# Attention with an off-by-one softmax, then a soft mixture of experts: the extra term of the denominator added by TensorE in PSUM, the half chunk of x stored without zero blocks, x transposed 448 wide, and q and k copied by ScalarE for every sixth pair

## The chip, the cores and the metric

The kernel runs on one core of one Trainium2 chip. That core has TensorE (PE in the profile, with its weight loads as PEld), VectorE (DVE), ScalarE (ACT), GpSimd (POOL) and SyncE (SP, which here only issues transfers). The metric is device microseconds for one execution. Lower is better.

## The reference, cut to what matters

```python
# q, k, v: batch 8, 12 heads, 448 tokens, 64 wide
scores = scale * q @ k.T
m = max(scores, -1);  e = exp(scores - m)
attn = e / (sum(e, -1) + exp(-m) + 1e-9)      # the off-by-one term is exp(-m)
x = (attn @ v), heads side by side            # 3584 tokens x 768
logits = x @ phi                              # 32 slots: 8 experts x 4
d = softmax(logits over all tokens);  slot_input = d.T @ x
slot_out[e] = relu(slot_input[e] @ w1[e]) @ w2[e]     # 768 -> 1024 -> 768
c = softmax(logits over the slots);  out = c @ slot_out
```

Each head has 448 tokens, which is three chunks of 128 and a half chunk of 64. Much of the kernel's shape, and of this change, comes from that half chunk.

## The kernel before

**Pairs.** The 96 heads are worked through as 48 pairs of heads, `s` or `n` from 0 to 47; a batch has six pairs, and three pairs are a group. The even head of a pair lies in partitions 0 to 63 and the odd one in 64 to 127. The order of all instructions on every engine is the order in which the Python lists them: there is no scheduler, and each engine works through its own list.

**One pair.** `T` (L214) transposes q and k into one PSUM tile with 28 transposes of 64x64, and ScalarE (L227) or VectorE (L229) copies the result to SBUF; which of them is set by `n < 6 or pl == 0`, where `pl` is the pair's place in its group. `A1` and `A` compute scores with the query in the partitions (L268, L256), and VectorE takes the maximum of each row (L270, L259). `W1` to `W3`, once a group, negate the maxima on GpSimd, transpose them on TensorE (L297, L298), copy them with ScalarE (L303), and compute exp(-m) into `ec` (L306, L309). `AB` and `Bk` compute the scores again with the key in the partitions (L354, L332), subtract the maximum by a second matmul into the same PSUM bank (L358, L335), and ScalarE exponentiates (L360, L338). `AB` also carries the `A1` matmuls of a later pair between its own. `AV` (L393) multiplies the exponentials with v, which has a column of ones behind its 64 columns, so each of the seven 65-wide results holds its own row sum in column 64. For the three full chunks of queries the stationary tile is 128x128; for the half chunk (`qs = [3]`) it is 128x64, the two heads going to the two halves of the PSUM partitions.

**Normalising.** `N1` (L405) copies the 455 columns to `ubuf`, on ScalarE for the first 44 pairs. `N2` adds 1e-9 and exp(-m) to the seven row sums with one VectorE instruction (L414), takes the reciprocal (L415), and GpSimd multiplies it into x: the three full chunks (L419), then for the half chunk a pair of masked reciprocals (L423) and a 128x128 product (L424). The mask makes a block in which each head's 64 columns are zero in the 64 partitions that belong to the other head. `PX` (L445) transposes x with four matmuls of 128x128, the last of them against `ident2`, two identities of 64 stacked, and ScalarE copies 512 columns to `xT` (L451).

**Per batch.** `P(b)` lists steps for the slot softmax that are put between the pairs of the next batch: `l_mm` (L471, logits: 6 parts of the model width by 4 chunks), `s_mm` (L539, slot inputs: 6 by 4 matmuls and 4 for the sums), a fade of the running sum when the maximum moves, and `c_turn` (L544 to L549), which stores the row softmax and the reciprocal of its sum. The last batch's steps, `last`, stand behind the pairs.

**One turn of the main loop** is, in TensorE's order: `AB(s,0)`, `AB(s,1)`, `AV(s-1)` for key chunks 2 and 3, a batch step, `AV(s-1)` for the half chunk of queries, `N1(s-1)`; then `AB(s,2)`, `Bk(s,3)`, `T(s+6)`, once a group `W2` and `W3`, `AV(s)` for key chunks 0 and 1, a batch step, `PX(s-2)`, `N2(s-1)`. All transfers from HBM are issued by GpSimd between its computations. Behind the pairs come the two expert layers, a selection, and 56 output matmuls (L793) whose results are scaled and stored. The tiles of the attention share one long SBUF tile `R`; expert weights are loaded over its parts once those are done with.

Of the kernel before, what the change touches and what calls it, by code (L numbers as in the profile page):

```python
# [25 lines left out]
NP = 3  # L26
# [5 lines left out]
def kernel(  # L32
# [35 lines left out]

    ident = const.tile([128, 128], BF16, name="ident")
    identf = const.tile([128, 128], F32, name="identf")  # L70
    ident2 = const.tile([128, 128], BF16, name="ident2")
# [3 lines left out]
    halfm = const.tile([128, 2], F32, name="halfm")  # L75

    NQK, NE, VPN, NATV = 7, 5, HG * 4 * VS, HG * 4 * D
    sizes = [("nq0", 2 * NP * S), ("nq1", 2 * NP * S), ("nv", NATV), ("qk6", 2 * S), ("wm1", 512),  # L80
             ("qk0", 2 * S), ("qk1", 2 * S), ("qk2", 2 * S), ("wm0", 512), ("qk3", 2 * S), ("vp0", VPN),
             ("qk4", 2 * S), ("x0", 4 * DD), ("qk5", 2 * S), ("e2", NE * 2 * S), ("e1", S), ("vp1", VPN),
             ("xT", KC * 512), ("x1", 4 * DD)]
    at_, n_ = {}, 0
    for nm, z in sizes:
        at_[nm] = n_
# [8 lines left out]
    xb = [part(f"x{i}", 0, 4 * DD).rearrange("p (i d) -> p i d", i=4) for i in range(2)]  # L95
    xT = part("xT", 0, KC * 512).rearrange("p (j s) -> p j s", j=KC)

    halves = [("w1", e) for e in range(E)] + [("w2", e) for e in range(E)]
    w_sb, w_col = {}, {}
# [43 lines left out]
    with ExitStack() as at:  # L143
# [33 lines left out]
        load(1, "k")  # L177


        for h in range(2):  # L180
            nc.vector.tensor_add(ident2[:, 64 * h:64 * h + 64], ident[:, 0:64], ident[:, 64:128])
        nc.vector.tensor_copy(identf, ident)
        nc.gpsimd.memset(sel, 0.0)
        for base in (0, 64):
# [5 lines left out]
        nc.vector.memset(halfm, 0.0)  # L190
        for hl in range(2):
            nc.vector.memset(halfm[64 - 64 * hl:128 - 64 * hl, hl:hl + 1], 1.0)
        for t in wm:
            nc.vector.memset(t, 0.0)
        for t in vp:
# [18 lines left out]
        def T(n):  # L214
            g, pl = divmod(n, NP)
            ps = psA.tile([128, 2, S], BF16, tag="a", name="ps_t")
            for a in range(2):
                src = nat["qk"[a], g]
                for tok in range(7):
                    for hl in range(2):  # L220

                        c = kcol(hl, tok) if a else (2 * tok if tok < 4 else 2 * tok - 7) * 64
                        r = slice(64 * hl, 64 * hl + 64)
                        nc.tensor.transpose(ps[r, a, c:c + 64], src[r, pl, tok * D:(tok + 1) * D], ident[r, r])  # L224
            t = qk_t[n % NQK]
            if n < 6 or pl == 0:
                nc.scalar.copy(t, ps)  # L227
            else:
                nc.vector.tensor_copy(t, ps)  # L229
            qkT[n] = t  # L230
# [62 lines left out]
        def W2(g):  # L293
            w = wm[g % 2]
            ps = pb_("ps_m")
            for i in range(3):
                nc.tensor.matmul(ps[:, i * 128:(i + 1) * 128], w[:, i, :], ident, start=True, stop=True)  # L297
            nc.tensor.matmul(ps[:, 384:448], w[:, 3, :], ident2[:, 0:64], start=True, stop=True)  # L298
            st["ps_m"] = ps

        def W3(g):
            t = psm.tile([128, S], BF16, tag="mT", name="mT")
            nc.scalar.copy(t, st["ps_m"][:, 0:S])  # L303
            mT[g] = t
            e = psm.tile([128, NP, 7], F32, tag="ec", name="ec", bufs=3)
            nc.scalar.activation(e[:, :, 0:6].rearrange("p l (i h) -> p i l h", i=3),  # L306
                                 ngm[g][:, 0:18].rearrange("p (i l h) -> p i l h", i=3, h=2),
                                 AF.Exp, scale=scale)
            nc.scalar.activation(e[:, :, 6], ngm[g][:, 18:21], AF.Exp, scale=scale)  # L309
            ec[g] = e  # L310


        def Bk(n, i, c=0):
# [94 lines left out]
        def N2(n):  # L408
            g, pl = divmod(n, NP)
            b, pb = divmod(n, PB)  # L410
            u = us[n]
            eng = nc.gpsimd if on_pool(n) else nc.vector
            rec = psm.tile([128, 7], F32, tag="rec", name="rec", bufs=3)
            nc.vector.scalar_tensor_tensor(rec, u[:, :, D], 1e-9, ec[mg(n)][:, pl, :], op0=ALU.add, op1=ALU.add)  # L414
            nc.vector.reciprocal(rec, rec)  # L415
            x = xb[b % 2]
            c = pb * 128
            rec2 = psm.tile([128, 2], F32, tag="rec2", name="rec2", bufs=3)
            eng.tensor_mul(  # L419
                x[:, 0:3, c:c + 128].rearrange("p i (h d) -> p i h d", h=2),  # L420
                u[:, 0:6, 0:D].rearrange("p (i h) d -> p i h d", h=2),
                rec[:, 0:6].rearrange("p (i h) -> p i h", h=2).unsqueeze(3).to_broadcast([128, 3, 2, D]))
            eng.tensor_scalar(rec2, halfm, rec[:, 6:7], None, op0=ALU.mult)  # L423
            eng.tensor_mul(  # L424
                x[:, 3, c:c + 128].rearrange("p (h d) -> p h d", h=2),
                u[:, 6, 0:D].unsqueeze(1).to_broadcast([128, 2, D]),
                rec2.unsqueeze(2).to_broadcast([128, 2, D]))

# [9 lines left out]
        def PX(n):  # L438
            b, pb = divmod(n, PB)
            x, c = xb[b % 2], slice(pb * 128, pb * 128 + 128)  # L440
            two = n == NPAIR - 1
            pss = [pb_("ps_x") for _ in range(1 + two)]
            for i in range(4):
                o = (i % 2 if two else i) * 128
                nc.tensor.matmul(pss[i // 2 if two else 0][:, o:o + 128], x[:, i, c], ident if i < 3 else ident2,  # L445
                                 start=True, stop=True)
            if two:
                nc.scalar.copy(xT[:, pb, 0:256], pss[0][:, 0:256])
                nc.vector.tensor_copy(xT[:, pb, 256:512], pss[1][:, 0:256])
            else:  # L450
                nc.scalar.copy(xT[:, pb, :], pss[0])  # L451

# [5 lines left out]
        def P(b):  # L458
# [7 lines left out]
            def l_mm(js):  # L466
                if js[0] == 0:
                    v["ps_l"] = pa([128, 4, NS], F32, "ps_l")
                for j in js:
                    for i in range(4):  # L470
                        nc.tensor.matmul(v["ps_l"][:, i, :], xT[:, j, i * 128:(i + 1) * 128], phi_sb[:, j, :],  # L471
                                         start=(j == 0 and i == 0), stop=(j == KC - 1), skip_group_check=True)

            def t_mm(js):
                if js[0] == 0:
                    v["ps_t"] = pa([128, 128], F32, "ps_lT")
                for j in js:
                    for i in range(4):
                        nc.tensor.matmul(v["ps_t"][32 * i:32 * i + 32, :], phi_sb[:, j, :],
                                         xT[:, j, i * 128:(i + 1) * 128], start=(j == 0), stop=(j == KC - 1),  # L480
                                         skip_group_check=True)

            def l_ev():
# [48 lines left out]
            def s_mm(j0=0, j1=KC + 1):  # L532
                ps = pa([128, j1 - j0, NS], F32, "ps_s")
                for j in range(j0, j1):
                    for i in range(4):

                        w = x[:, i, j * 128:(j + 1) * 128] if j < KC else \
                            ones[:, int(i == 3):int(i == 3) + 1].to_broadcast([128, 128])
                        nc.tensor.matmul(ps[:, j - j0, :], w, v["cd"][:, 4 + i, :], start=(i == 0), stop=(i == 3))  # L539
                v["ps_s"] = ps  # L540

            def c_turn():
                ps = pa([128, 128], BF16, "ps_ct")
                nc.tensor.transpose(ps, flat(v["cd"][:, 0:4, :]), ident)  # L544
                nc.vector.tensor_copy(cT[:, b // 2, :, b % 2, :], ps.rearrange("p (h j) -> p h j", h=2))
                r = crec[:, b, :]
                nc.vector.reduce_sum(r, v["cd"][:, 0:4, :], axis=AX.X)
                nc.vector.tensor_scalar(r, r, 1e-9, None, op0=ALU.add)
                nc.vector.reciprocal(r, r)  # L549

            def s_add():
                if b:
# [82 lines left out]
        for s in range(NPAIR):  # L635
            for y in range(2):
# [40 lines left out]
                if y == 0:  # L677
                    if 0 <= s - 1:
                        for i in range(4):
                            AV(s - 1, i, [3])  # L680
                        N1(s - 1)
                        if not on_pool(s - 1):
                            N2(s - 1)
                else:
                    if 0 <= s - 1 and on_pool(s - 1):
                        N2(s - 1)
# [34 lines left out]
        for i in range(3):  # L721
            AV(n, i, [3])
        AV(n, 3, range(4))
        load_second(0, 4)
        N1(n)
        N2(n)
# [160 lines left out]
```

## Time and profile before

| What | Value |
|---|---|
| Median of 3 runs | 311.84 us (309.37 to 312.33) |
| The profiled execution's own time | 310.7 us |
| Its span, first to last instruction | 308.9 us |
| Mean granted TensorE clock | 0.964 |
| TensorE busy / weight loads busy | 275.6 us (89%) / 159.0 us (51%) |
| VectorE busy | 257.2 us (83%) |
| ScalarE busy | 249.3 us (81%) |
| GpSimd busy | 202.7 us (66%) |

A busy time is the union of an engine's instruction intervals. The end of a matmul in the trace is modelled and includes its way through the array, so that two matmuls overlap in the rows; what a matmul costs in a row of them is read from the distance between their starts. That distance is called a slot in the prediction. "128\*64" in a row is the stationary tile, rows by columns; "128x65" is the result.

### The profile page before, as it was taken

To read this page: it belongs to the slowest core of one execution; us is meant where nothing else is said; L and a number is where in the kernel's file an instruction comes from. 1 tells how busy PE (TensorE), PEld (TensorE's weight loads), DVE (VectorE), ACT (ScalarE), POOL (GpSimd) and SP (SyncE) were. 2 spreads that over 40 slices of the span, in tenths; PEclk is the share of its full clock that TensorE was granted. 3 is DMA by queue.
4 is the path that set the end of the run, shared out by engine and by line. 5 is a ranking of instruction groups with operands and counts; after the bars stand their busy time and mean duration, and the time that the engine had idled before them with its cause. 6 is when DMAs were issued, how large, how long until landed. Compare 5 with 4: busy or idle time off the path is not lost.

```text
span 308.9 us, 12205 instructions
## 1 busy us (share of the span) xinstructions
PE 275.6 (89%) x5067; PEld 159.0 (51%) x5068; DVE 257.2 (83%) x607; ACT 249.3 (81%) x549; POOL 202.7 (66%) x403
## 2 busy tenths in 40 slices
PE   2899999999999999999999999999999899994810
PEld 1434456565666656665566566656665556451200
DVE  4778999999999999999999999999999566536930
ACT  2357599999999999999999999999999997236810
POOL 8682769788788878896889788879584863000000
PEclk9999999999999999999999999999999999999555
DMA  6999499999999999999999999999971999937997
GB/s 88 149 128 202 64 205 150 198 182 205 163 196 157 210 169 198 155 203 149 149 164 186 177 186 169 196 177 203 166 110 17 144 126 204 337 128 260 415 439 312
DMA packets 49350, 57.44 MB, mean 186 GB/s; under 512 B 2832, under 2 KB 41488, under 8 KB 48912
## 3 DMA queue, kind: packets, MB, share of 16 engines
q0 software_dynamic: 45536, 42.52, 90.1%
q1 hardware_dynamic: 3760, 14.16, 11.5%
q8 instruction: 39, 0.64, 0.8%
q14 instruction: 15, 0.12, 0.1%
HBM read 88.18 MB, written 14.16 MB: 331 GB/s over the span
## 4 chain that ended last, share of the span: by engine, by line
PE 50%; DVE 30%; ACT 7%; issue 4%; POOL 4%; DMA 1%; DVEq 0%; POOLq 0%
DVE mx L270 15%; PE ps_av L393 11%; PE ps_a L268 6%; PE ps_t L224 6%; PE ps_b L354 5%; PE ps_b L358 4%; DVE mx L250 3%; DVE mx L259 3%; PE ps_b L332 3%; PE ps_a L246 2%; DVE W L801 2%; DVE R L229 2%; PE ps_x L445 2%; ACT R L227 2%; PE ps_so L764 2%
## 5 line engine op out<-in xcount | busy, mean ns | idle before, releaser
L270 DVE TENSOR_REDUCE mx<-ps_a 128x1 f32<-128x448 f32 x248 | 136.6, 613 | 5.3 <-PE ps_a L268 5.1
L360 ACT ACTIVATE R<-ps_b 128x448 bf16<-128x448 f32 x272 | 131.0, 573 | 1.1 <-PE ps_b L358 0.8
L268 PE MATMUL ps_a<-R 64*128 64x448 bf16 x248 | 80.5, 352 | 1.8 <-DVE mx L270 1.8
L354 PE MATMUL ps_b<-R 64*128 64x448 bf16 x272 | 73.9, 353 | 0.9
L358 PE MATMUL ps_b<-mT,sel 64*128 64x448 bf16 x272 | 70.6, 350 | 0.0
L393 PEld LDWEIGHTS <-R 128*128 128x128 bf16 (+1 forms) x1536 | 50.5, 101 | 30.5 <-issue 26.4
L393 PE MATMUL ps_av<-R 128*128 128x65 bf16 (+1 forms) x1536 | 64.9, 196 | 0.1
L419 POOL TENSOR_TENSOR R<-ubuf,rec 128x384 bf16<-128x384 f32 x44 | 36.3, 825 | 37.9 <-DVE rec L415 23.4
L224 PEld LDWEIGHTS <-R 64*64 64x64 bf16 x1344 | 31.1, 113 | 19.2 <-issue 7.8
L338 ACT ACTIVATE R<-ps_b 128x448 bf16<-128x448 f32 x64 | 36.0, 579 | 5.9 <-PE ps_b L335 5.9
L224 PE MATMUL ps_t<-ident,R 64*64 64x64 bf16 x1344 | 32.0, 198 | 5.9 <-DMA R<-in_q_dram 4.3
L451 ACT CAST R<-ps_x 128x512 bf16<-128x512 f32 x47 | 28.1, 598 | 5.7 <-PE ps_x L445 5.7
L259 DVE TENSOR_REDUCE mx<-ps_a 128x1 f32<-128x448 f32 x48 | 29.6, 616 | 0.6 <-PE ps_a L256 0.3
L358 PEld LDWEIGHTS <-sel 64*128 64x128 bf16 x272 | 21.5, 94 | 14.9 <-issue 5.3
L268 PEld LDWEIGHTS <-R 64*128 64x128 bf16 x248 | 23.1, 94 | 9.8
L405 ACT COPY ubuf<-ps_av 128x455 f32<-128x455 f32 x44 | 25.2, 573 | 3.0 <-PE ps_av L393 2.8
L227 ACT COPY R<-ps_t 128x896 bf16<-128x896 bf16 x20 | 18.4, 922 | 11.3 <-PE ps_t L224 11.0
L250 DVE TENSOR_REDUCE mx<-ps_a 128x1 f32<-128x448 f32 x40 | 22.6, 618 | 4.3 <-PE ps_a L246 3.9
L332 PE MATMUL ps_b<-R 64*64 64x448 bf16 (+1 forms) x112 | 22.7, 386 | 0.0
L335 PE MATMUL ps_b<-mT,sel 64*64 64x448 bf16 (+1 forms) x112 | 21.5, 366 | 0.0
L424 POOL TENSOR_TENSOR R<-ubuf,rec 128x128 bf16<-128x128 f32 x44 | 17.5, 398 | 3.7
L354 PEld LDWEIGHTS <-R 64*128 64x128 bf16 x272 | 17.2, 94 | 4.7 <-issue 0.2
(132 smaller groups left out, 454.0 us busy)
## 6 DMA issues: line engine op xcount, KB each, us to landing
W<-in_moe_w_dram POOLq DMA_DIRECT2D x22, 768.0 KB, 9.5
R<-in_v_dram POOLq DMA_DIRECT2D x32, 192.0 KB, 4.6
out_dram<-W SPq DMA_DIRECT2D x2, 2688.0 KB, 10.3
R<-in_q_dram POOLq DMA_DIRECT2D x15, 336.0 KB, 7.4
R<-in_k_dram POOLq DMA_DIRECT2D x15, 336.0 KB, 8.5
wd<-in_moe_w_dram POOLq DMA_DIRECT2D x8, 384.0 KB, 10.0
R<-wd SPq DMA_DIRECT2D x8, 384.0 KB, 8.6
R<-in_moe_w_dram POOLq DMA_DIRECT2D x2, 768.0 KB, 8.3
```

The lines of the kernel that those rows point to most:

```text
L224: nc.tensor.transpose(ps[r, a, c:c + 64], src[r, pl, tok * D:(tok + 1) * D], ident[r, r])
L250: nc.vector.reduce_max(mx[g][:, c:c + 1], pss[hl][:, 0:S], axis=AX.X)
L259: nc.vector.reduce_max(mx[g][:, c:c + 1], ps[:, 0:S], axis=AX.X)
L268: nc.tensor.matmul(ps[:, 0:S], t[r, 0, i * 128:(i + 1) * 128], t[r, 1, :], start=True, stop=True)
L270: nc.vector.reduce_max(mx[g][:, c:c + 1], ps[:, 0:S], axis=AX.X)
L332: nc.tensor.matmul(outs[hl], t[rs[hl], 1, cols], t[rs[hl], 0, :], start=True, stop=False)
L338: nc.scalar.activation(e, p[:, 0:S], AF.Exp, scale=scale)
L354: nc.tensor.matmul(ps[hl][:, 0:S], t[rs[hl], 1, cols], t[rs[hl], 0, :], start=True, stop=False)
L358: nc.tensor.matmul(ps[hl][:, 0:S], sel[rs[hl], h:h + 1].to_broadcast([64, 128]), mT[mg(n)][rs[hl], :], start=False, stop=True)
L360: nc.scalar.activation(e[:, hl, :], ps[hl][:, 0:S], AF.Exp, scale=scale)
L393: nc.tensor.matmul(o, eT[n, i, hl][:, qc], vp[g % 2][:, 2 * pl + hl, i, 0:W65], start=(i == 0 and u == 0 and hl == 0), stop=(i == 3), skip ...
L419: eng.tensor_mul(x[:, 0:3, c:c + 128].rearrange("p i (h d) -> p i h d", h=2), u[:, 0:6, 0:D].rearrange("p (i h) d -> p i h d", h=2), rec[: ...
```

## The change

Seven edits, made together:

1. `N2` no longer adds exp(-m). A new function `D1` adds it in PSUM: two f32 matmuls per pair with the f32 identity as the stationary tile, one moving the six columns of the full chunks, one the column of the half chunk, accumulated onto the row sums that `AV` left there. It stands between the last `AV` of a pair and its `N1`.
2. `W3` computes exp(-m) with one ScalarE instruction in place of two, and GpSimd adds 1e-9 to it.
3. The half chunk of x is stored 64 wide with no zeros (`xh`), by one GpSimd instruction in place of two.
4. Where that half chunk is the stationary operand it is now taken as two tiles: in `PX` and `s_mm` two 64x64 ones in place of one 128x128; in `l_mm` the 64 columns of `xT` twice as 128x64, once for each half of the PSUM partitions. `t_mm` moves the 64 columns twice.
5. `xT` is 448 wide in place of 512, and ScalarE copies 448 columns.
6. q and k of a pair are copied by ScalarE when `n % 6 == 0` (was: `n % 3 == 0`), else by VectorE, from pair 6 on.
7. The 1e-9 and the reciprocal of `c_turn` are done once for all batches, behind the pairs. Constants that only the mask needed are gone, and the parts of `R` move a little (a pad of 352 keeps what follows in its place within 32 elements).

```diff
-             ("qk4", 2 * S), ("x0", 4 * DD), ("qk5", 2 * S), ("e2", NE * 2 * S), ("e1", S), ("vp1", VPN),
-             ("xT", KC * 512), ("x1", 4 * DD)]
+             ("qk4", 2 * S), ("x0", 7 * DD // 2), ("pad", 352), ("qk5", 2 * S), ("e2", NE * 2 * S), ("e1", S), ("vp1", VPN),
+             ("xT", KC * S), ("x1", 7 * DD // 2)]
...
-            if n < 6 or pl == 0:
+            if n < 6 or n % 6 == 0:
                 nc.scalar.copy(t, ps)
...
-            e = psm.tile([128, NP, 7], F32, tag="ec", name="ec", bufs=3)
-            nc.scalar.activation(e[:, :, 0:6].rearrange("p l (i h) -> p i l h", i=3),
-                                 ngm[g][:, 0:18].rearrange("p (i l h) -> p i l h", i=3, h=2),
-                                 AF.Exp, scale=scale)
-            nc.scalar.activation(e[:, :, 6], ngm[g][:, 18:21], AF.Exp, scale=scale)
+            e = psm.tile([128, 21], F32, tag="ec", name="ec", bufs=3)
+            nc.scalar.activation(e, ngm[g], AF.Exp, scale=scale)
+            nc.gpsimd.tensor_scalar(e, e, 1e-9, None, op0=ALU.add)
             ec[g] = e
+
+        def D1(n):
+            pl, e = n % NP, ec[mg(n)]
+            d = av[n][:, 0:7 * W65].rearrange("p (s c) -> p s c", c=W65)[:, :, D]
+            nc.tensor.matmul(d[:, 0:6].rearrange("p (i h) -> p i h", h=2), identf,
+                             e[:, 0:18].rearrange("p (i c) -> p i c", i=3)[:, :, 2 * pl:2 * pl + 2],
+                             start=False, stop=True, skip_group_check=True)
+            nc.tensor.matmul(d[:, 6:7], identf, e[:, 18 + pl:19 + pl], start=False, stop=True, skip_group_check=True)
...
-            nc.vector.scalar_tensor_tensor(rec, u[:, :, D], 1e-9, ec[mg(n)][:, pl, :], op0=ALU.add, op1=ALU.add)
-            nc.vector.reciprocal(rec, rec)
+            nc.vector.reciprocal(rec, u[:, :, D])
...
-            eng.tensor_scalar(rec2, halfm, rec[:, 6:7], None, op0=ALU.mult)
-            eng.tensor_mul(
-                x[:, 3, c:c + 128].rearrange("p (h d) -> p h d", h=2),
-                u[:, 6, 0:D].unsqueeze(1).to_broadcast([128, 2, D]),
-                rec2.unsqueeze(2).to_broadcast([128, 2, D]))
+            eng.tensor_scalar(xh[b % 2][:, pb, :], u[:, 6, 0:D], rec[:, 6:7], None, op0=ALU.mult)
...
-            for i in range(4):
+            for i in range(3):
                 o = (i % 2 if two else i) * 128
-                nc.tensor.matmul(pss[i // 2 if two else 0][:, o:o + 128], x[:, i, c], ident if i < 3 else ident2,
+                nc.tensor.matmul(pss[i // 2 if two else 0][:, o:o + 128], x[:, i, c], ident, start=True, stop=True)
+            for hl in range(2):
+                r, o = slice(64 - 64 * hl, 128 - 64 * hl), 128 if two else 384
+                nc.tensor.matmul(pss[-1][64 * hl:64 * hl + 64, o:o + 64], xh[b % 2][r, pb, :], ident[r, r],
                                  start=True, stop=True)
...
-                nc.scalar.copy(xT[:, pb, :], pss[0])
+                nc.scalar.copy(xT[:, pb, :], pss[0][:, 0:S])
...
-                    for i in range(4):
-                        nc.tensor.matmul(v["ps_l"][:, i, :], xT[:, j, i * 128:(i + 1) * 128], phi_sb[:, j, :],
-                                         start=(j == 0 and i == 0), stop=(j == KC - 1), skip_group_check=True)
+                    for i in range(5):
+                        r = slice(0, 128) if i < 3 else slice(64 * i - 192, 64 * i - 128)
+                        nc.tensor.matmul(v["ps_l"][r, min(i, 3), :], xT[:, j, 128 * min(i, 3):min(128 * i + 128, S)],
+                                         phi_sb[:, j, :], start=(j == 0 and i == 0), stop=(j == KC - 1),
+                                         skip_group_check=True)
...
+                        if j < KC and i == 3:
+                            for hl in range(2):
+                                r = slice(64 - 64 * hl, 128 - 64 * hl)
+                                nc.tensor.matmul(ps[64 * hl:64 * hl + 64, j - j0, :], xh[b % 2][r, j, :],
+                                                 v["cd"][r, 7, :], start=False, stop=True, skip_group_check=True)
+                            continue
...
-                nc.vector.tensor_scalar(r, r, 1e-9, None, op0=ALU.add)
-                nc.vector.reciprocal(r, r)
...
                         for i in range(4):
                             AV(s - 1, i, [3])
+                        D1(s - 1)
                         N1(s - 1)
...
         AV(n, 3, range(4))
+        D1(n)
         load_second(0, 4)
...
         last[3]()
+        nc.vector.tensor_scalar(crec, crec, 1e-9, None, op0=ALU.add)
+        nc.vector.reciprocal(crec, crec)
```

More of the change, by code (lines that the diff above doesn't have):

```diff
@@ L70 @@
     identf = const.tile([128, 128], F32, name="identf")
-    ident2 = const.tile([128, 128], BF16, name="ident2")
+    ident2 = const.tile([128, 64], BF16, name="ident2")
     ones = const.tile([128, 2], BF16, name="ones")
@@ L74 @@
     phi_sb = const.tile([128, KC, NS], BF16, name="phi_sb")
-    halfm = const.tile([128, 2], F32, name="halfm")
     NQK, NE, VPN, NATV = 7, 5, HG * 4 * VS, HG * 4 * D
@@ L94 @@
     wm = [part(f"wm{i}", 0, 512).rearrange("p (i c) -> p i c", i=4) for i in range(2)]
-    xb = [part(f"x{i}", 0, 4 * DD).rearrange("p (i d) -> p i d", i=4) for i in range(2)]
-    xT = part("xT", 0, KC * 512).rearrange("p (j s) -> p j s", j=KC)
+    xb = [part(f"x{i}", 0, 3 * DD).rearrange("p (i d) -> p i d", i=3) for i in range(2)]
+    xh = [part(f"x{i}", 3 * DD, DD // 2).rearrange("p (j d) -> p j d", d=D) for i in range(2)]
+    xT = part("xT", 0, KC * S).rearrange("p (j s) -> p j s", j=KC)
     halves = [("w1", e) for e in range(E)] + [("w2", e) for e in range(E)]
@@ L177 @@
         load(1, "k")
-        for h in range(2):
-            nc.vector.tensor_add(ident2[:, 64 * h:64 * h + 64], ident[:, 0:64], ident[:, 64:128])
+        nc.vector.tensor_add(ident2, ident[:, 0:64], ident[:, 64:128])
         nc.vector.tensor_copy(identf, ident)
@@ L189 @@
                 pattern=[[-1, HG]], channel_multiplier=1)
-        nc.vector.memset(halfm, 0.0)
-        for hl in range(2):
-            nc.vector.memset(halfm[64 - 64 * hl:128 - 64 * hl, hl:hl + 1], 1.0)
         for t in wm:
@@ L297, in W2 @@
                 nc.tensor.matmul(ps[:, i * 128:(i + 1) * 128], w[:, i, :], ident, start=True, stop=True)
-            nc.tensor.matmul(ps[:, 384:448], w[:, 3, :], ident2[:, 0:64], start=True, stop=True)
+            nc.tensor.matmul(ps[:, 384:448], w[:, 3, :], ident2, start=True, stop=True)
             st["ps_m"] = ps
@@ L413, in N2 @@
             rec = psm.tile([128, 7], F32, tag="rec", name="rec", bufs=3)
-            nc.vector.scalar_tensor_tensor(rec, u[:, :, D], 1e-9, ec[mg(n)][:, pl, :], op0=ALU.add, op1=ALU.add)
-            nc.vector.reciprocal(rec, rec)
+            nc.vector.reciprocal(rec, u[:, :, D])
             x = xb[b % 2]
             c = pb * 128
-            rec2 = psm.tile([128, 2], F32, tag="rec2", name="rec2", bufs=3)
             eng.tensor_mul(
@@ L448, in PX, with xt @@
                 nc.scalar.copy(xT[:, pb, 0:256], pss[0][:, 0:256])
-                nc.vector.tensor_copy(xT[:, pb, 256:512], pss[1][:, 0:256])
+                nc.vector.tensor_copy(xT[:, pb, 256:S], pss[1][:, 0:S - 256])
             else:
-                nc.scalar.copy(xT[:, pb, :], pss[0])
+                nc.scalar.copy(xT[:, pb, :], pss[0][:, 0:S])
+        def xt(j, i):
+            if i < 3:
+                return xT[:, j, i * 128:(i + 1) * 128]
+            return xT[:, j, 384:S].unsqueeze(1).to_broadcast([128, 2, 64])
         lb = [keep.tile([128, 5, NS], F32, name=f"lb{i}") for i in range(2)]
@@ L479, in t_mm @@
                         nc.tensor.matmul(v["ps_t"][32 * i:32 * i + 32, :], phi_sb[:, j, :],
-                                         xT[:, j, i * 128:(i + 1) * 128], start=(j == 0), stop=(j == KC - 1),
+                                         xt(j, i), start=(j == 0), stop=(j == KC - 1),
                                          skip_group_check=True)
@@ L535, in s_mm @@
                     for i in range(4):
+                        if j < KC and i == 3:
[4 more added lines that the diff above has]
+                            continue
                         w = x[:, i, j * 128:(j + 1) * 128] if j < KC else \
                             ones[:, int(i == 3):int(i == 3) + 1].to_broadcast([128, 128])
-                        nc.tensor.matmul(ps[:, j - j0, :], w, v["cd"][:, 4 + i, :], start=(i == 0), stop=(i == 3))
+                        nc.tensor.matmul(ps[:, j - j0, :], w, v["cd"][:, 4 + i, :], start=(i == 0), stop=(i == 3),
+                                         skip_group_check=True)
                 v["ps_s"] = ps
```

## The prediction, made before the changed kernel was run

> **What bounds the kernel now.** I began with the page's busy shares and its chain of the work that ended last.
>
> ```profile
> PE 275.6 (89%) x5067; PEld 159.0 (51%) x5068; DVE 257.2 (83%) x607; ACT 249.3 (81%) x549; POOL 202.7 (66%) x403
> ...
> PE 50%; DVE 30%; ACT 7%; issue 4%; POOL 4%; DMA 1%; DVEq 0%; POOLq 0%
> ```
>
> Three engines are nearly full, and half of the chain is TensorE. The chain repeats: a VectorE maximum behind the logits' step starts at 156.57, 186.43 and 216.29 us, so six pairs take 29.86 us. The window view of one such batch (columns: PE, PEld, DVE, ACT, POOL busy) shows all three at 96% or more:
>
> ```profile
> 185.21:215.07 29.86, 29.35 (x599) 18.24 (x595) 28.56 (x69) 28.57 (x67) 25.45 (x50) 1.00 1.18 186
> ```
>
> To see what TensorE needs when nothing holds it up, I read a stretch in which the chain is TensorE alone (chain in order of time: start, us, what):
>
> ```profile
> 180.27 0.72 PE ps_av L393 x20
> 180.99 0.29 PE ps_a L268
> 181.28 0.19 PE ps_b L354 x2
> ...
> 182.16 0.47 PE ps_t L224 x28
> 182.62 0.47 PE ps_av L393 x12
> 183.09 0.22 PE ps_x L445 x4
> 183.31 0.29 PE ps_a L268
> ...
> 184.75 0.47 PE ps_av L393 x12
> 185.21 0.60 PE ps_l L471 x24
> ```
>
> One pair, from one group of AV to the next, is 184.75 - 180.27 = 4.48 us. Six are 26.9. The rest of a batch, from the starts in the timeline: the maxima's transposes twice 0.21, the logits 0.68 (below), the slot inputs 0.70 (77.62 to 78.32), the f32 transpose 0.14, two single transposes 0.07 each: 2.1. So TensorE needs 29.0 of the 29.86 us, and has 0.9 us a batch to spare. **TensorE's instruction slots are the bound**; whatever is added to them beyond 0.9 us a batch is paid.
>
> **What a slot costs.** The timeline of TensorE gives starts:
>
> ```profile
> 62.17 0.63 PE L224 MATMUL ps_t<-ident,R 64*64 64x64 bf16 x28
> 62.74 0.54 PE L393 MATMUL ps_av<-R 128*128 128x65 bf16 x12
> 63.11 0.39 PE L445 MATMUL ps_x<-ident,R 128*128 128x128 bf16 x4
> 63.43 0.36 PE L268 MATMUL ps_a<-R 64*128 64x448 bf16 x1
> ...
> 65.23 0.75 PE L471 MATMUL ps_l<-phi_sb,R 128*128 128x32 bf16 x24
> 65.91 0.32 PE L393 MATMUL ps_av<-R 128*64 128x65 bf16 x8
> 66.17 0.36 PE L268 MATMUL ps_a<-R 64*128 64x448 bf16 x1
> ```
>
> Where the shape of the stationary tile stays the same, slots are short: 12 AV in 63.11 - 62.74 = 0.37 us (31 ns each), and the chain gives the 24 logit matmuls 0.60 (25 ns each). But from the first logit matmul to the first 128\*64 one is 65.91 - 65.23 = 0.68: **0.08 more when the shape changes**. The same at 128\*128 to 64\*128: four PX at 55 ns are 0.22 (the chain's figure), and the next shape starts after 0.32, so 0.10 more; and at 128\*64 to 64\*128: eight AV at 31 to 35 ns a pair (two run together in the two column halves, like T's) are 0.13 to 0.14, the next starts after 0.26, 0.12 more. At 64\*64 to 128\*128: another T has 28 transposes left at 177.44 and 17 at 177.62, 16 ns each, so 28 are 0.46, and AV starts after 0.57, 0.11 more. I take 0.095 us for one change of shape.
>
> **The change part by part, on TensorE.**
>
> *D1's place.* It sits behind AV's 128\*64 tiles and before AB's 64\*128 ones, and is 128\*128 itself. Before: one change of shape. After: two. +0.095 a pair.
>
> *D1's passes.* The trace has f32 matmuls in two places:
>
> ```profile
> 158.33 0.30 PE L496 MATMUL ps_lT<-identf,lb 128*128 128x128 f32 x1
> 158.47 0.33 PE L445 MATMUL ps_x<-ident,R 128*128 128x128 bf16 x3
> ...
> 276.25 0.30 PE L831 MATMUL ps_cs<-crec,identf 64*64 64x16 f32 x8
> ```
>
> L831 is four matmuls in the code and eight in the trace: an f32 matmul runs as two passes, each with its own load of weights. D1 is two matmuls, so four passes. Their price is not in the trace for 128\*128 with 6 or 1 columns. Lower end: the shortest slot there is, 25 ns. Upper end: the f32 transpose at L496, 128 columns, 158.47 - 158.33 = 0.14. Between: the eight passes of L831 start in two bursts of four, by the code one for each quarter of the array. The load rows, 0.13 us each, run 0.15 us for the first four and 0.21 for all eight, so the second burst starts some 0.055 us after the first. These load 64 columns, D1 loads 128, so twice that, 0.11, is my value (an estimate). It lies nearest to the L496 row, which is the same f32 128\*128 load. D1 = 0.095 + 4 x 0.11 = 0.535 us, between 0.195 and 0.655. 48 pairs: **25.7 us** (9.4 to 31.4).
>
> [...]
>
> *PX.* Three 128\*128 matmuls, a change of shape, two 64\*64 that run together like T's (0.03), the same exit as before: 0.095 + 0.03 - 0.055 = +0.07 a pair, **3.4 us**.
>
> *Logits.* Per part of the width: three at 25 ns, change, two 128\*64 together (0.03), change back. A batch: 6 x (0.075 + 0.03) + 11 x 0.095 = 1.68, against 0.68: +1.0. The last change falls away, since AV's 128\*64 tiles follow. Seven batches and the last: **8 us**.
>
> *Slot inputs.* 6 x 0.105 + 12 x 0.095 + 0.10 for the sums = 1.87, against 0.70: +1.17. Eight batches: **9.4 us**. The last of them stand between the last exponentials and the expert layer, where nothing else runs.
>
> Sum of what TensorE gets: 25.7 + 3.4 + 8 + 9.4 = 46.5 us.
>
> **What hides it.** 0.9 us a batch of spare time, over the 6.8 batches from 42 to 245 us: 6.1. In the first 42 us TensorE waits for VectorE, ScalarE and transfers between pairs, so D1 and PX of five pairs (5 x 0.6) are covered: 3. Net 46.5 - 9.1 = **+37.4 us**.
>
> **The other engines** only lose work, or have room. VectorE loses L414 (161 ns x48; some 0.1 of it is its own slot) and seven times L548 and L549 in the pairs, and takes seven copies more (0.53 each in the chain): about -0.5 us a batch. ScalarE loses seven copies (0.80 in the chain), one exp a group (0.2 x17), and 64 columns of L451 (from 448 columns in 537 ns at L303 to 512 in 598: 0.06 each): -1.5 us a batch. GpSimd loses L423 (292 ns) and half of L424 (398 ns for 128 columns), about 0.45 us a pair, and gains 0.27 a group. With TensorE further ahead as the bound, none of this is on the path: priced at zero; were VectorE the bound it would be worth 0.5 x 6.8 = 3.4 us. The added wait, GpSimd's 1e-9 behind ScalarE's exp, stands in GpSimd's queue ahead of the next L419; that row already waits 1.67 us at that point (173.25 to 174.92) and D1 uses the result more than a pair later. D1 holds back N1 by 0.5 us, and behind N1 on ScalarE wait AB's next exponentials, which TensorE delivers later by the same amount. No transfer changes in size but for its place in R, and no queue is reordered.
>
> **Sum.** The profiled execution took 310.7 us (span 308.9, 1.8 around it), 0.4% below the median of the runs shown. 310.7 + 37.4 = **348 us**.
>
> **Rivals.**
>
> *Faster: TensorE is not the bound.* Place: the pair loop. If the matmul rows only look full because they overlap, the added slots fill idle time, VectorE stays the bound, and its relief gives 310.7 - 3.4 = 307 us. It decides if TensorE's real spare time exceeds the 5.8 us which a batch gains (6 x 0.605 + 1.0 + 1.17). For it: PEld is busy only 51%. Against: 4.48 us per pair is measured between starts, not busy time, and leaves 0.9. Chance 0.05; and 0.03 that gains and costs meet within 1%, which is about what a measurement of this kernel can tell from no change. [...]
>
> *No price for changing shape in these spots*, because the two half tiles begin while the full ones finish. Then D1's passes alone remain: 48 x 0.44 = 21.1, PX 48 x -0.025 = -1.2, less 9.1: 310.7 + 10.8 = 322 us. For it: packed tiles do overlap each other at T and AV. Against: all four kinds of change above cost 0.08 to 0.12. Chance 0.08.
>
> *The delay of N1 backs up*: D1 between AV and N1 keeps the single AV bank and ScalarE idle, and neither the spare time nor the early cover is usable: with 0.14 a pass 310.7 + 46.5 + 5.7 = 363 us. Chance 0.08.
>
> *Cheap passes*, 25 ns each, changes paid: 46.5 - 16.3 - 9.1 = 21.1, 332 us; this is the lower end of the forecast's own range, whose upper end is 354 at 0.14. The forecast with that range has 0.76.
>
> Range: 322 to 361, which leaves out the faster and even cases and the backed-up one (0.16). Faster by over 1%: 0.05; within 1%: 0.03; slower: 0.92.
>
> **What would show it.** Right: a batch of 34 to 35 us in place of 29.86; VectorE and ScalarE below 85% in it; L309 and L312 as four passes over some 0.5 us between AV and L268; 0.08 to 0.12 at each step between full and half tiles in the logits and slot inputs, whose groups take 1.7 and 1.9 us. Wrong: logits still at 0.7 us (no change of shape paid), passes at 25 ns, or a batch below 31 us with TensorE still full, which would mean that the spare time was misread.

## The result, and the profile after

The changed kernel takes 353.04 us (median of 4 runs, 351.73 to 353.70); the kernel before takes 311.19 beside it. The ratio is 1.135, with a 95% interval of 1.128 to 1.142: 42 us slower. The profiled execution took 351.73 us (span 350.0), 41.0 more than the one before; the prediction had 37.4.

The page's busy shares and chain, as shown of the kernel before:

```profile
PE 321.7 (92%) x5404; PEld 202.5 (58%) x5404; DVE 255.0 (73%) x544; ACT 247.4 (71%) x525; POOL 195.8 (56%) x376
...
PE 87%; DVE 6%; ACT 1%; issue 1%; DMA 1%; DVEq 0%; POOLq 0%
```

VectorE, ScalarE and GpSimd each have less to do in all than before (255.0, 247.4 and 195.8 us against 257.2, 249.3 and 202.7), and TensorE has 46 us more. TensorE was half of the chain that ended last; it is now 87% of it. The window view of one batch, from one logits group to the next (columns: stretch, length, then busy PE, PEld, DVE, ACT, POOL, then the granted clock, the share of the DMA engines and GB/s):

```profile
208.15:242.73 34.58, 34.58 (x639) 23.52 (x636) 28.64 (x62) 28.15 (x63) 24.35 (x46) 1.00 1.05 163
```

A batch takes 34.58 us in place of 29.86. TensorE is occupied in all of it. VectorE's and ScalarE's busy times are about what they were (28.56 and 28.57), so their shares fall to 83% and 81%.

One pair in the chain in order of time (start, us, what), to be held against the stretch from 180.27 to 184.75 of the kernel before:

```profile
197.66 0.72 PE ps_av L395 x20
198.38 0.32 PE ps_av L309 x2
198.69 0.22 PE ps_av L312 x2
198.91 0.29 PE ps_a L264
...
201.01 0.17 PE ps_x L441 x3
201.18 0.15 PE ps_x L444 x2
...
202.75 0.72 PE ps_av L395 x20
```

It takes 202.75 - 197.66 = 5.09 us, against 4.48. D1 is L309 and L312: two matmuls in the code, four passes here, 0.54 us between AV and the next pair's scores. PX is 0.32 where it was 0.22. The timeline of TensorE (start, us, line, operation, operands, tile) shows the logits:

```profile
208.15 1.91 PE L476 MATMUL ps_l<-phi_sb,R 128*128 128x32 bf16 x30
209.91 0.30 PE L395 MATMUL ps_av<-R 128*64 128x65 bf16 x8
210.13 0.39 PE L309 MATMUL ps_av<-ec,identf 128*128 128x6 f32 x2
210.38 0.36 PE L312 MATMUL ps_av<-ec,identf 128*128 128x1 f32 x2
210.67 0.36 PE L264 MATMUL ps_a<-R 64*128 64x448 bf16 x1
```

The 30 logit matmuls hold TensorE from 208.15 to 209.91, 1.76 us; 24 took 0.68 before. Six matmuls more, of 25 ns each elsewhere, cannot be a whole microsecond: the rest is spent between full and half tiles. The slot inputs show it group by group:

```profile
188.54 0.23 PE L551 MATMUL ps_s<-cd,R 128*128 128x32 bf16 x3
188.70 0.20 PE L546 MATMUL ps_s<-cd,R 64*64 64x32 bf16 x2
188.84 0.24 PE L551 MATMUL ps_s<-cd,R 128*128 128x32 bf16 x3
189.01 0.20 PE L546 MATMUL ps_s<-cd,R 64*64 64x32 bf16 x2
```

Three full and two half tiles come round every 0.30 us (188.54 to 188.84), where four full tiles took 0.10.

By stages, from the starts of the logits groups in both traces: up to the first group 65.2 us became 68.3 (+3.1); from the first to the seventh 177.0 became 206.1 (+29.1); from there to the last group 18.2 became 22.9 (+4.7); from the last group to the end 48.5 became 52.6 (+4.1).

### The profile page after: what moved, and what is told of

Same layout as the page of the kernel before. It is cut to its first block, busy times and chain, and to the rows that moved or that the text cites. A ratio compares the mean times of both kernels' runs of the same rounds, so it can differ in the third digit from the quotient of the medians.

```text
span 350.0 us, 12710 instructions
## 1 busy us (share of the span) xinstructions
PE 321.7 (92%) x5404; PEld 202.5 (58%) x5404; DVE 255.0 (73%) x544; ACT 247.4 (71%) x525; POOL 195.8 (56%) x376
## 3 DMA queue, kind: packets, MB, share of 16 engines
q1 hardware_dynamic: 3760, 14.16, 10.2%
## 4 chain that ended last, share of the span: by engine, by line
PE 87%; DVE 6%; ACT 1%; issue 1%; DMA 1%; DVEq 0%; POOL 0%; POOLq 0%
PE ps_av L395 16%; PE ps_a L264 11%; PE ps_b L356 8%; PE ps_b L360 7%; PE ps_t L220 7%; PE ps_av L309 4%; PE ps_b L334 4%; PE ps_l L476 4%; DVE mx L246 3%; PE ps_av L312 3%; PE ps_b L337 3%; PE ps_s L551 3%; PE ps_x L441 2%; PE ps_h L761 2%; PE ps_o L808 2%; PE ps_x L444 2%
## 5 line engine op out<-in xcount | busy, mean ns | idle before, releaser
L266 DVE TENSOR_REDUCE mx<-ps_a 128x1 f32<-128x448 f32 x248 | 139.4, 618 | 23.7 <-PE ps_a L264 20.7
L362 ACT ACTIVATE R<-ps_b 128x448 bf16<-128x448 f32 x272 | 128.7, 552 | 2.4 <-PE ps_b L360 1.9
L450 ACT CAST R<-ps_x 128x448 bf16<-128x448 f32 x47 | 25.4, 540 | 25.6 <-PE ps_x L444 25.0
L340 ACT ACTIVATE R<-ps_b 128x448 bf16<-128x448 f32 x64 | 34.1, 548 | 6.2 <-PE ps_b L337 6.2
L407 ACT COPY ubuf<-ps_av 128x455 f32<-128x455 f32 x44 | 23.8, 541 | 12.8 <-PE ps_av L312 8.3
L360 PEld LDWEIGHTS <-sel 64*128 64x128 bf16 x272 | 23.5, 94 | 11.6 <-issue 3.2
L255 DVE TENSOR_REDUCE mx<-ps_a 128x1 f32<-128x448 f32 x48 | 29.5, 615 | 0.7 <-PE ps_a L252 0.6
L264 PEld LDWEIGHTS <-R 64*128 64x128 bf16 x248 | 23.2, 94 | 6.0
L303 POOL TENSOR_SCALAR ec<-ec 128x21 f32<-128x21 f32 x17 | 4.8, 280 | 39.0 <-ACT ec L302 38.9
L246 DVE TENSOR_REDUCE mx<-ps_a 128x1 f32<-128x448 f32 x40 | 22.5, 617 | 5.3 <-PE ps_a L242 5.3
L225 DVE COPY R<-ps_t 128x896 bf16<-128x896 bf16 x35 | 21.5, 614 | 0.2 <-PE ps_t L220 0.2
L356 PEld LDWEIGHTS <-R 64*128 64x128 bf16 x272 | 17.9, 94 | 3.9
## 6 DMA issues: line engine op xcount, KB each, us to landing
out_dram<-W SPq DMA_DIRECT2D x2, 2688.0 KB, 10.2
```

Source lines behind the costliest of these rows:

```text
L246: nc.vector.reduce_max(mx[g][:, c:c + 1], pss[hl][:, 0:S], axis=AX.X)
L264: nc.tensor.matmul(ps[:, 0:S], t[r, 0, i * 128:(i + 1) * 128], t[r, 1, :], start=True, stop=True)
L266: nc.vector.reduce_max(mx[g][:, c:c + 1], ps[:, 0:S], axis=AX.X)
L340: nc.scalar.activation(e, p[:, 0:S], AF.Exp, scale=scale)
L356: nc.tensor.matmul(ps[hl][:, 0:S], t[rs[hl], 1, cols], t[rs[hl], 0, :], start=True, stop=False)
L360: nc.tensor.matmul(ps[hl][:, 0:S], sel[rs[hl], h:h + 1].to_broadcast([64, 128]), mT[mg(n)][rs[hl], :], start=False, stop=True)
```

## The experiments

The theory is that TensorE's slots bound the pair loop, and that the change adds two kinds: f32 passes at 0.11 us and changes of tile shape at about 0.1. The rivals are that the time went into D1's wait (N1 on ScalarE cannot start before it), into the extra matmuls as such, or into the granted clock, whose mean fell from 0.964 to 0.945.

**D1 taken out of the changed kernel.**

```diff
-        nc.vector.reciprocal(rec, u[:, :, D])
+        nc.vector.scalar_tensor_tensor(rec, u[:, :, D], 1e-9, ec[mg(n)][:, pl, :], op0=ALU.add, op1=ALU.add)
+        nc.vector.reciprocal(rec, rec)
...
-                        D1(s - 1)
```

> The changed kernel with edits 1 and 2 undone: VectorE adds exp(-m) again (two exps, one extra VectorE instruction a pair), no D1; the half tiles and all else stay. Theory (TensorE's slots are the bound): D1 takes 0.540 us of slots a pair in the changed kernel's trace, so a batch falls from 34.58 to 31.3 us or a little above, and the time from 353 by up to 25.9 to 327 to 331 us. Rival (the granted clock, 0.945 in place of 0.964, made a good part of the loss): the time falls by far less, to 340 or above.

Measured: 329.61 us (ratio to the kernel before 1.059, 1.055 to 1.064), 23.4 less than the changed kernel. Most batches take 32.1 us, 0.8 above the 31.3 expected: of the 3.24 us of slots that went, 0.7 turned into waits. In the profiled execution (331.39 us) the mean clock is 0.948, much like the changed kernel's, so the clock is not what separates the two.

**D1 alone on the kernel before.** The same lines the other way round, with W3's single exp.

> The kernel before with D1 alone (and W3's single exp, GpSimd's 1e-9), VectorE's addition taken out; zero blocks stay. Theory: 29.0 us of slots a batch plus 6 x 0.54 is 32.2 in place of 29.86; over the run 311 + 25.9 - 6 of spare time - 3 of early cover = 326 to 330 us. Rival (TensorE had more room than the starts say, or the half tiles alone did it): 311 to 316 us.

Measured: 331.37 us (1.064, 1.060 to 1.067), 20.0 more than the kernel before; a batch takes 32.46 us. A little above the range: the theory holds, but less was hidden than I had granted D1. A batch got 6 x 0.54 = 3.24 us and became 2.60 longer, so 0.64 was hidden and not 0.9; and the stretch up to the first logits group, with seven pairs' D1 (3.8 us) in it, went from 65.2 to 67.9, so it covered 1.1 and not 3.

D1 alone (+20.0) and the rest alone (+18.2, from the run without D1) make 38.2, and both together 41.9. The batches do not show that difference: 2.60 for D1 and 2.20 for the rest make 4.80, and both together made 4.72. Where the medians' 3.7 us lie is open; the stretches at half clock, of which more below, are a candidate.

**Logits and slot inputs grouped by tile shape.**

```diff
-                for j in js:
-                    for i in range(5):
+                for j, i in [(j, i) for j in js for i in range(3)] + [(j, i) for j in js for i in (3, 4)]:
...
                 for j in range(j0, j1):
-                    for i in range(4):
...
-                        if j < KC and i == 3:
...
+                    for i in range(4 if j == KC else 3):
...
+                for j in range(j0, min(j1, KC)):
+                    for hl in range(2):
...
```

> The changed kernel, but the logits and the slot inputs do all full tiles first and then all half tiles: two changes of shape in place of 11 and 12 a batch, the same number of matmuls. Theory (changes of shape are paid, some 0.1 us each): 9 or 10 changes fewer in each, 1.9 us a batch, a batch at 32.7 us and the time at 353 - 14 = 339 us (337 to 341). Rival (the extra matmuls cost, not the change of shape): no change, 353 us.

Measured: 334.60 us (1.075, 1.071 to 1.079), 18.4 less than the changed kernel, with the same matmuls in another order; 337 to 341 was expected, so it gained more than forecast. The batch fell to 32.6 us, as expected (two timeline rows of that run):

```profile
199.22 0.90 PE L475 MATMUL ps_l<-phi_sb,R 128*128 128x32 bf16 x30
199.97 0.30 PE L395 MATMUL ps_av<-R 128*64 128x65 bf16 x8
```

The 30 logit matmuls now take 0.75 us where they took 1.76. Ten changes of shape fewer are 1.01 us, 0.10 each. This settles that it is the change of shape and not the number of matmuls. In the traces the time between the first and the last logits group gives 14.4 of it, the stretch behind the last group 1.9 and the one ahead of the first 0.6; the medians lie 1.6 further apart than the two profiled executions.

**D1's passes kept, its use taken away.** The passes write spare columns of AV's bank, and VectorE adds the term as before.

```diff
-            d = av[n][:, 0:7 * W65].rearrange("p (s c) -> p s c", c=W65)[:, :, D]
+            d = av[n][:, 456:463]
```

> The changed kernel, but D1's four passes write spare columns of the same PSUM bank that nobody reads, and VectorE adds exp(-m) as before; N1 need not wait for D1 then. The passes do no useful work. Theory (the slots cost, not the wait): 353 us, at most 2 less. Rival (the cost is N1's wait for D1 and what stands behind N1 on ScalarE): the time falls towards that of the kernel without D1, 327 to 340 us.

Measured: 354.26 us (1.138, 1.134 to 1.143). But the trace shows that N1 was still released by D1's last matmul (L314 there; 8.5 of the 12.8 us that ScalarE idled ahead of N1 ended with it): both use one PSUM tile, and in this program the wait is for the tile. So this run does not separate slot from wait, and only says that VectorE's extra instruction cost nothing that can be told beside a full TensorE (354.26 us against 353.04). The separation came with this one, whose passes go to a bank of the scores:

```diff
+            st["pre"] = d = pb_("ps_b")
+            nc.tensor.matmul(d[:, 448:454], identf, e[:, 7 * pl:7 * pl + 6], start=True, stop=True, skip_group_check=True)
+            nc.tensor.matmul(d[:, 454:455], identf, e[:, 7 * pl + 6:7 * pl + 7], start=True, stop=True, skip_group_check=True)
...
-                ps[hl] = pb_("ps_b")
+                ps[hl] = st.pop("pre", None) or pb_("ps_b")
```

> Again passes that do no useful work, since in the run before them N1 was still released by them (they shared its tile): the same four f32 passes at the same place, now into the unused columns of the score bank that the next AB overwrites, so that N1 waits for AV alone; VectorE adds exp(-m) as before. 45 of 48 pairs have them. Theory (the slots cost, not N1's wait): 350 to 354 us. Rival (N1's wait and ScalarE's queue behind it cost): towards the 329.6 us without D1, 330 to 342 us.

Measured: 351.58 us (1.130, 1.122 to 1.138). The group rows of N1's copy (busy and mean ns, then the idle time ahead of it and its releasers) in the changed kernel:

```profile
L407 ACT COPY ubuf<-ps_av 128x455 f32<-128x455 f32 x44 | 23.8, 541 | 12.8 <-PE ps_av L312 8.3 <-POOL ngm L273 2.3 <-POOL R L378 0.9
```

and in this run:

```profile
L409 ACT COPY ubuf<-ps_av 128x455 f32<-128x455 f32 x44 | 25.2, 572 | 1.0 <-PE ps_av L397 1.0
```

The 8.3 us of waiting for D1 are gone; what is left, 1.0, is for AV (L397 here). The time is the same within 1.5 us, with 45 of the 48 sets of passes in place. **The wait cost nothing; the slots cost.**

**D1 ahead of the half chunk's AV**, so that its 128x128 passes follow 128x128 tiles.

```diff
+                        D1(s - 1)
                         for i in range(4):
                             AV(s - 1, i, [3])
-                        D1(s - 1)
```

> The changed kernel with D1 ahead of the half chunk's AV in place of behind it, so that its 128x128 f32 passes follow AV's 128x128 tiles and one change of shape a pair is saved in 47 of 48 pairs. Theory: 47 x 0.095 = 4.5 us less than 353, so 348 to 349 us. Rival (D1's cost is its passes alone, the change of shape at its entry is hidden by their loads): 353 us.

Measured: 348.09 us (1.119, 1.112 to 1.125), 5.0 less than the changed kernel, where 4.5 was expected. Over 47 pairs that is 0.106 us for one change of shape; by the batch, 34.12 us in place of 34.58, it is 0.08.

**D1 in bf16.**

```diff
-            e = psm.tile([128, 21], F32, tag="ec", name="ec", bufs=3)
+            e = psm.tile([128, 21], BF16, tag="ec", name="ec", bufs=3)
             nc.scalar.activation(e, ngm[g], AF.Exp, scale=scale)
-            nc.gpsimd.tensor_scalar(e, e, 1e-9, None, op0=ALU.add)
...
-            nc.tensor.matmul(d[:, 0:6].rearrange("p (i h) -> p i h", h=2), identf,
+            nc.tensor.matmul(d[:, 0:6].rearrange("p (i h) -> p i h", h=2), ident,
...
```

> The changed kernel with D1 in bf16 (exp(-m) and the identity; the 1e-9, which bf16 cannot hold beside a term near 1, and GpSimd's instruction for it are left out): two matmuls with short slots in place of four f32 passes. Theory (the f32 passes at 0.11 us are the larger part of D1): D1 falls from 0.54 to 0.10 + 0.055, 48 x 0.385 = 18.5 us less than 353, so 333 to 336 us. Rival (the place of D1 between AV and N1 matters, not the type): no more than 5 us less.

Measured: 332.79 us (1.072, 1.068 to 1.075), 20.2 less than the changed kernel and just below the range expected. The timeline of TensorE in that run:

```profile
197.20 0.30 PE L394 MATMUL ps_av<-R 128*64 128x65 bf16 x8
197.43 0.18 PE L308 MATMUL ps_av<-ec,ident 128*128 128x6 bf16 x1
197.47 0.16 PE L311 MATMUL ps_av<-ec,ident 128*128 128x1 bf16 x1
197.57 0.36 PE L264 MATMUL ps_a<-R 64*128 64x448 bf16 x1
```

Each matmul is one pass, and D1 holds TensorE from 197.43 to 197.57, 0.14 us in place of 0.54, with the wait of N1 still there. 48 x 0.40 = 19.2 of the 20.2 measured.

**All three repairs together** (bf16, ahead, grouped).

> All three together on the changed kernel: D1 in bf16, ahead of the half chunk's AV, and the logits and slot inputs grouped by tile shape. Theory: from the 334.6 us of the grouped version, 48 x (0.54 - 0.055) = 23.3 us less, less what VectorE and ScalarE then hold up: 311 to 316 us, no faster than the kernel before, since two changes of shape a batch in each group and one in PX stay. Rival (what the other engines save shows once TensorE's slots are cheap again): 306 us or below.

Measured: 314.01 us (1.013, 1.008 to 1.018). Of 42 us, three edits that leave the arithmetic of the change in place (but for bf16 in a term beside a sum, and the 1e-9) take back 39. It is no faster than the kernel before, as expected. The next version has the same D1 and the same edits 6 and 7, but keeps the zero blocks, and takes 307.77 us: even grouped, the half tiles cost some 6 us more than the zeros that they avoid.

**What is worth keeping: zero blocks, with a cheap D1.** The kernel before with D1 in bf16 ahead of the half chunk's AV and one exp a group (`ident` for `identf` and the order above), and with edits 6 and 7 besides.

> The kernel before, zero blocks and all, with D1 in bf16 ahead of the half chunk's AV, one exp a group, ScalarE's copies at every sixth pair, and the reciprocals of the row sums taken at the end. TensorE gets 48 x 0.055 = 2.6 us, 0.33 a batch, and VectorE and ScalarE lose work. Theory (TensorE needs 29.0 + 0.33 of 29.86 us a batch): 309 to 312 us, no change that can be told. Rival (VectorE was as much a bound as TensorE): 306 to 308 us.

Measured: 307.77 us (0.992, 0.989 to 0.995): 0.8% below the kernel before. Its interval leaves out 1, but the difference is under the 1% that I take for what can be told. The value lies in the rival's range and not in the theory's, so some of what VectorE and ScalarE save may reach the end when TensorE is less loaded; that is not shown. To see which half would do it, two versions with five rounds each:

> The 307.8 us version (zero blocks, D1 in bf16 ahead of the half chunk's AV, one exp a group) without the two other edits: ScalarE copies q and k of every third pair again and the reciprocals of the row sums are taken in each batch. If D1 is what gains, by taking an instruction off VectorE in every pair: 307 to 309 us. If the copies and the reciprocals gain: 310 to 311 us.

Measured: 309.35 us (0.997, 0.994 to 1.000).

> The kernel before with only those two other edits: ScalarE copies at every sixth pair, reciprocals once at the end. No D1. VectorE gets 7 copies of 0.53 us more and some 14 short instructions less. If D1 is what gains: 310 to 312 us. If these two gain: 308 us.

Measured: 309.56 us (0.998, 0.995 to 1.001). Both lie between the two values expected. Neither half stands out from no change, and which of them gains in the version with both, if either does, is left open.

**The half clock at the end.** In the changed kernel's trace the granted clock is 0.50 from 301.4 to 308.2 us, in the last batch's steps, where the kernel before has 1.00.

```diff
         PX(n)
+        keep_busy(2)
         last[2]()
...
-   lambda: keep_busy(1), s_max
+   lambda: keep_busy(2), s_max
```

> The changed kernel with three more 512-wide matmuls of the identity that nobody reads, put where TensorE waits in the last batch's steps: two behind the last PX, one more ahead of the last maximum. They fit in waits of 0.4 us each and change no result. Theory (the granted clock falls to half at 301.4 us because TensorE idles and runs short slots there): the clock stays at 1.0 and the run is 2 to 4 us shorter, 349 to 351 us. Rival (the half clock there has another cause): 353 to 354 us, and the clock's row shows half again.

Measured: 352.49 us (1.138, 1.135 to 1.141), 0.5 below the changed kernel and inside its runs' spread. The windows of its trace:

```profile
298.00:301.40 3.40, 3.40 (x57) 2.13 (x55) 0.89 (x4) 0.76 (x3) 0.00 (x0) 1.00 1.03 287
301.40:304.90 3.50, 2.99 (x39) 1.99 (x39) 1.46 (x5) 0.43 (x2) 0.00 (x0) 1.00 0.87 337
304.90:308.30 3.40, 3.40 (x36) 1.34 (x40) 1.37 (x7) 0.76 (x2) 0.00 (x0) 0.50 0.64 230
```

Half of the slow stretch went (301.4 to 304.9 is at full clock again), the other half stayed, and the time hardly moved. The half that stayed lies on the first 48 matmuls of the expert layer, which take 4.30 us here, 4.12 in the changed kernel and 2.70 in the kernel before. That the extra matmuls moved the stretch is not shown: it lasts 3.4 us also in the run with D1's passes set free of N1, which has no such matmuls, and 10.2 us in the run with D1's use taken away, whose last steps are those of the changed kernel. Nor is it shown that the clock could be had back for a gain.

## Why the prediction was right

*The bound.* Right. I had 29.0 us of slots in a batch of 29.86; the batch came out at 34.58 (34 to 35 forecast), full of TensorE. From the slots measured now, a batch got 6 x (0.54 + 0.09) + 1.08 + 1.24 = 6.1 us more and became 4.7 longer, so the spare time was 1.4, not 0.9, and the 29.0 were nearer to 28.5. D1 and the half tiles, each undone or done alone, are worth 18 to 23 us, and VectorE's saved work did not show. The rival that TensorE had room fell with the run of D1 alone.

*D1.* Right in place and size: 0.54 us against 0.535. The four passes start 0.133, 0.112 and 0.112 us apart, and the next pair's scores start 0.183 after the last of them, a pass and 0.07 more. My 0.11 was twice the spacing in the 64-column row at L831 (0.055 us), and the measured row is where that doubling led; that the spacing goes with the columns loaded rests on these two rows, and no run varied the columns.

*Change of shape.* Right: 0.095 taken; 0.10 by the grouped logits and by D1's move. The way back from half to full tiles is a little dearer (half tile to full in 0.13, full to half in 0.105, where a full tile alone takes 0.025), which makes the logits 1.76 and the slot inputs 1.94 us in place of the 1.68 and 1.87 forecast, and PX +0.09 in place of +0.07.

*What hides it.* The term that was mis-sized, in both of its parts, and the two errors pull opposite ways. Spare time gave 1.4 us a batch rather than 0.9, so 9.5 in place of 6.1. It lay in the second scores: summed from start to start over one batch, all matmuls into `ps_b` take 10.31 us in the kernel before and 9.00 in the changed one, with the same matmuls, and outside the changed parts no other group differs by more than 0.05. So 1.3 us of that were waits, which the added slots used up; with D1 alone, or the rest alone, it is 9.68 us, and half of the waits are left. Early cover was less than the 3 us put down: ahead of the first logits group stand seven pairs' D1 and six pairs' PX, 7 x 0.54 + 6 x 0.09 = 4.3 us, and that stage grew by 3.1, so it covered 1.2 (a stretch at half clock lies in it).

From the first to the seventh logits group the prediction's own terms give 6 x (5.8 - 0.9) = 29.4 us, and 29.1 was measured. That this is so close is partly luck: the slots were larger and the spare time too, and one stretch at half clock made up the rest. The whole sum was 3.6 us short, and that shows ahead of these batches and behind them.

What the sum lacked is the clock. Between the first and the last logits group there is one stretch at half clock (window rows of the changed kernel):

```profile
141.00:144.40 3.40, 3.40 (x58) 2.81 (x54) 2.21 (x6) 1.99 (x6) 0.76 (x3) 0.50 1.17 200
...
102.91:137.58 34.67, 34.65 (x640) 23.61 (x637) 28.66 (x62) 28.16 (x63) 23.89 (x45) 1.00 1.00 155
137.58:173.56 35.98, 35.98 (x639) 24.58 (x636) 28.79 (x62) 28.21 (x63) 24.01 (x46) 0.95 0.95 140
```

The batch that holds it took 35.98 us beside 34.67 for the one ahead of it: 1.3 us. Another lies at 28.4 to 31.8, in the first stage. The one at 301.4 to 308.2 covers the last slot inputs and the first 48 matmuls of the expert layer (two timeline rows of the kernel before, then two of the changed one):

```profile
265.88 2.77 PE L748 MATMUL ps_h<-W,ubuf 128*32 128x512 bf16 x48
268.58 0.23 PE L544 MATMUL ps_ct<-ident,cd 128*128 128x128 bf16 x1
...
305.33 4.19 PE L761 MATMUL ps_h<-W,ubuf 128*32 128x512 bf16 x48
309.45 0.23 PE L557 MATMUL ps_ct<-ident,cd 128*128 128x128 bf16 x1
```

The same 48 matmuls take 4.12 us from start to start in place of 2.70, 1.4 more. Behind the last logits the run is 4.1 us longer; the slots added there, 1.08 + 1.24, and these 1.4 make 3.7 of them. The run with D1 ahead of the half chunk's AV points to a price of the same size: its one execution at a mean clock of 0.959 took 344.55 us, the three at 0.944 to 0.945 took 348.04 to 348.66. Other runs do not show it as plainly (with D1's use taken away, the execution at 0.955 took 353.56, those at 0.941 to 0.946 took 351.95 to 355.10), and no run set the clock. So the clock's part, some 3 us, is worked out and not tested.

*The other engines.* Right: what they saved was worth nothing in the changed kernel; with VectorE's addition given back (and D1's passes still run), the stretch from the sixth logits group to the seventh took 31.74 us (242.28 to 274.02) against 31.70 (242.73 to 274.43). Where TensorE is less loaded, the version with the cheap D1 and both other edits came out 0.8% lower, and whether that is their gain is open.

*The rivals.* No price for a change of shape: refuted by the grouped order (18.4 us) and by D1's move (5.0). N1's wait backing up: refuted by the run in which N1 waits for AV alone. Cheap f32 passes: refuted by the rows, and by bf16's 20.2 us.

*The weight-load share.* PEld's 51% was the argument for the rival that TensorE has room. In the changed kernel's batch PEld is busy 23.52 of 34.58 us, 68%, and the experiments find no room there. The measure that held here was the distance between starts: the logit matmuls at 185.05 us of the kernel before start 25 ns apart, while the row of each lasts 176 ns.

## What to carry to other kernels

Read what a matmul costs from the distance between starts, and look for the places where the shape of the stationary tile changes: each was 0.1 us here, four times a short matmul. Three full and two half tiles took 0.30 us where four full ones took 0.10, so halving a tile inside a loop cost eight times the 0.025 us of the zero-padded tile that it replaced. Group matmuls by tile shape (18.4 us here), and put an added one beside neighbours of its own shape (5.0). An f32 matmul of six columns or one against a 128x128 identity cost two passes, whose starts lay 0.11 to 0.13 us apart; in bf16 the six-column one cost one slot of 0.04. Before moving such a term to an engine one should ask whether that engine is the full one.

## What was not expected of the hardware

In the traces of eight versions, all of them with half tiles, the granted clock fell to 0.50 for 3.4, 6.8 or 10.2 us somewhere ahead of the half clock that every version shows at its end; the mean clock of those executions was 0.945 to 0.959. D1 alone with the zero blocks (0.965), and all three repairs together (0.961), had no such stretch. Between the first and the last logits group it happened in three of the eight, with TensorE busy in all of the 3.4 us, and some 2.7 to 3.6 us after a logits group had begun: 141.0 after 137.6 in the changed kernel and 141.1 after 137.5 in the run with more matmuls at the end; 103.9 after 101.2 and 209.7 after 206.9 in the run with D1's passes set free of N1, whose batches at those places took 36.1 us in place of 34.6. Other batches of the same order kept the full clock (1.00 from 102.91 to 137.58 in the changed kernel). What brings such a stretch about is not shown.
